# Delta-rule attention and a leaky-ReLU block on one Trainium2 core: corner blocks turned by VectorE transposes instead of DRAM bounces, inverses made for pairs of blocks, weights converted 768 columns at a time

## The chip, the cores and the metric

One core of one Trainium2 chip runs the whole program; the core has a matmul engine (PE, with its weight loads PEld), VectorE (DVE), ScalarE (ACT), GpSimd (POOL) and SyncE (SP), which issues most DMAs. The metric is the device time of one execution, in microseconds.

## The reference

```python
# q, k, v: (4, 8, 768, 48) float32; beta: (4, 8, 768); w_in (384, 2048), w_out (2048, 384) float64
k_n = k / (norm(k) + 1e-6)
for t in range(S):                        # S = 768 steps, state is 48 x 48 per sequence and head
    y[t]  = q[t] @ state
    v_old = k_n[t] @ state
    state = state + beta[t] * outer(k_n[t], v[t] - v_old)
x = y.transpose(0, 2, 1, 3).reshape(3072, 384)
h = x @ w_in
out = maximum(0.01 * h, h) @ w_out
```

## The kernel before, in words

The 768 steps are cut into 12 blocks of 64 steps, n = 0 to 11. In a block the recurrence over 64 steps is solved as a triangular system, so that all of it becomes matmuls; the 4 x 8 = 32 sequences and heads of a block are called lanes here. They are handled in two groups, g = 0 and 1. For each block there are these stages, each a Python generator, and `weave` writes their instructions in turns; a scheduler that plays the program against a timeline of its own then sets the final order on each engine.

- `gram(n)` (L175): loads keys and queries, transposed, into `kq` (two buffers, so g = 0 and g = 1 each have one), multiplies keys by keys and keys by queries on PE into `pg` (L201), copies the key products to `gs` on ACT (L205), and writes the masked query products to `rq` on DVE (L216). Each 64 x 64 product has two 32 x 32 diagonal corners and one corner below them. `gm` takes the lower corner (L220). The diagonal corners are written to DRAM (`gd`, 8 DMAs a block, L209) and read back into `L` (L224), which puts a lane and a half on each partition and the 32 x 32 corner along the free dimension.
- `inv(b)` (L272): inverts the corners on DVE. A memset clears `T` (L280), `norms` makes the key norms with a short Newton chain (L239 to L248) and scales `L` (L292), and `eliminate` (L253) goes through 31 columns, each with a multiply into `tmp` (L263) and a subtraction from `T` (L268), each in two parts. Blocks 0 and 1 are inverted together (64 + 64 partitions); from block 2 on each block alone uses the 128 partitions, with the columns split over two halves. The result goes back to the layout of the matmuls through DRAM: ACT makes a turned copy `Tt` (L299), DMAs write `td` and `tt` (L307, L308).
- `merge(n, g)` (L312): DMAs read `td` into `rt` and `tt` into `gm` (L318, L320); then two rounds of 32 x 32 matmuls, `pz` (L334) and `pu` (L342), give the lower corner of the inverse.
- `solve(n)` (L354): loads `rk`, `rv`, `rq` (L366, L367), scales `rv` by the norms on DVE (L388), and runs `pk` (L383), `pw` (L396), the state update `pc` (L404) and the output `py` (L414), each followed by copies on ACT. `columns(n)` (L435) turns the output into `px` (L443) and splits it into a high and a low part, `xh` on ACT and `xl` on DVE (L116).
- `ffn(n)` (L448): for each of 16 slices f of the 2048 columns 9 matmuls into `ph` (L468), leaky ReLU on ACT twice (`gh` L472, in place L473), the low part `gl` on DVE (L475), and 6 matmuls into `po` (L458), which run two slices behind. At the end `ob` is copied (L487) and stored (L490).
- `weights()` (L127): the weights come as float64. Each of 32 pieces of 384 columns (16 slices, two matrices) is turned into a high and a low part with two operations on ACT (L146, L160) and seven on DVE: four TENSOR_SCALARs (L148, L154, L156, L158) and three SCALAR_TENSOR_TENSORs (L155, L157, L161). Six pieces are written into the program ahead of the first inverse (KA = 6), the others behind it, and the last of them run beside the first block's `ffn`.

Every engine runs its instructions in the order given; DVE holds the inverse, the weights, `gl`, `rq` and more in one queue, and PE holds all matmuls in one queue. `weave` puts `solve(n+1)`, `inv(n+2)` and `gram(n+3)` beside `ffn(n)`.

Of the kernel before, what the change touches and what calls it, by code (L numbers as in the profile page):

```python
# [47 lines left out]
def delta_moe_kernel(ctx: ExitStack, tc, kqT, kv, qT, beta, cst, w_all, out, nblk):  # L48
# [65 lines left out]
    def split(src, hi, lo):  # L114
        nc.scalar.copy(hi, src)
        nc.vector.tensor_tensor(lo, src, hi.bitcast(F32), ALU.subtract)  # L116

    def load_w(k, gate=None):
        if k < 2 * NFC:
            raws[k] = raw = sb.tile([P, DO], U64, tag=f"w{k}", name=f"wr{k}", bufs=1)  # L120
            if gate:
                with behind(gate):
                    nc.vector.memset(raw[:, 0:1].bitcast(F32), 0.0)
            with behind("L"):
                nc.sync.dma_start(raw, w_all[:, k // 2, k % 2])

    def weights():  # L127
# [3 lines left out]
        for k in range(2 * NFC):  # L131
            f, x = k // 2, k % 2
            words = raws.pop(k).bitcast(F32).rearrange("p (n two) -> p two n", two=2)
            lo, hi = words[:, 0], words[:, 1]
            loi, hii = lo.bitcast(U32), hi.bitcast(U32)
            g = sb.tile([P, DO], F32, tag="cg", name=f"cg{k}", bufs=CB)
            r = sb.tile([P, DO], F32, tag="cr", name=f"cr{k}", bufs=1)
            gi, ri = g.bitcast(U32), r.bitcast(U32)

            def final():  # L140
                t = sb.tile([P, 2 * DO], F32R, tag=f"w{k}", name=f"w{k}", bufs=1)
                for e in range(2):
# [455 lines left out]
```

## Time and profile before

| What | Value |
|---|---|
| Runs of the kernel | 725.08, 725.47, 725.88 us; median 725.47 |
| Span of the profiled execution, first to last instruction | 722.7 us; the runs' median is 2.8 us above it |
| PE / DVE / ACT / POOL busy | 625.2 / 499.3 / 323.5 / 7.3 us |
| First matmul of `pz`, of `ph` | 77.37 us, 95.83 us |
| First copy of `ob` (end of block 0), of block 1 | 172.46 us, 212.73 us |
| Last copy of `ob` | 717.11 us |

Rows of a timeline give the start, the duration, the engine, the line, the operation, its tile and shape and how many were merged, and in brackets how long the engine had stood idle before and whom it waited for. Rows of a table by stage give the busy time of PE, PEld, DVE, ACT and POOL with the number of instructions, then the granted clock of the matmul engine, the DMA share and GB/s. Rows of the groups give line, engine, operation, tiles, shape and count, then busy time, the mean of one in ns, and the idle time before them.

### The profile page before, as it was taken

What the parts mean: (1) busy time and instruction counts of PE and PEld (TensorE: products, weight loads), DVE (VectorE), ACT (ScalarE), POOL (GpSimd) and SP (SyncE); (2) the same over time, 40 slices, a digit from 0 to 9 for tenths busy, and PEclk for the clock granted to TensorE, in tenths of its full rate; (3) what the DMA queues carried; (4) which work ended last, traced back from release to release, by engine and by line L of the source; (5) the groups of instructions that cost most, each with busy time, mean ns of one, the idle gap of its engine ahead of it and who ended that gap; (6) DMA issues with size and microseconds to landing.
All of it is one profiled execution on the core that took longest, in us unless ns stands there. A gap on an engine that the chain in (4) does not pass through costs nothing.

```text
span 722.7 us, 20972 instructions
## 1 busy us (share of the span) xinstructions
PE 625.2 (87%) x8296; PEld 580.9 (80%) x8296; DVE 499.3 (69%) x2222; ACT 323.5 (45%) x830; POOL 7.3 (1%) x12
## 2 busy tenths in 40 slices
PE   4200689978996999999999999999999999999996
PEld 4200569967995998988989999989989989999996
DVE  7988998999594856956955947847758559531211
ACT  3211554733453453554454544534634635544332
POOL 4000000000000000000000000000000000000000
PEclk9999978988997999999999999999999999999999
...
GB/s 239 102 271 107 177 206 131 59 115 23 46 14 128 85 57 164 4 68 154 3 98 124 3 128 95 15 136 73 32 142 49 50 129 2 68 24 2 3 20 23
DMA packets 130786, 60.91 MB, mean 84 GB/s; under 512 B 115392, under 2 KB 118592, under 8 KB 130688
## 3 DMA queue, kind: packets, MB, share of 16 engines
...
q8 instruction: 65, 1.06, 0.6%
...
## 4 chain that ended last, share of the span: by engine, by line
PE 65%; DVE 18%; DMA 7%; ACT 4%; SPq 3%; issue 3%; ACTq 0%; DVEq 0%
PE ph L468 26%; PE po L458 23%; PE pw L396 3%; PE pk L383 3%; DVE rq L216 3%; DMA tt<-T 3%; DVE rv L388 2%; DVE T L268 2%; PE pu L342 2%; DVE tmp L263 2%; DMA wr<-in_w_all 2%; PE py L414 2%; PE pz L334 2%; PE px L443 1%; SPq L307 1%
## 5 line engine op out<-in xcount | busy, mean ns | idle before, releaser
L468 PE MATMUL ph<-xh,w 128*128 128x256 f32 x1152 | 255.6, 295 | 11.4 <-DVE gl L475 8.2
L468 PEld LDWEIGHTS ph<-xh,w 128*128 128x128 f32 x1152 | 195.1, 192 | 22.5 <-DVE gl L475 11.4
L458 PE MATMUL po<-w,gh 128*128 128x384 f32 x768 | 188.0, 342 | 2.4 <-ACT gh L472 2.4
L475 DVE TENSOR_TENSOR gl<-ph,gh 128x256 fp32r<-128x256 f32 x192 | 80.4, 422 | 132.4 <-ACT ph L473 123.4
L468 PE MATMUL ph<-xl,w 128*128 128x256 f32 x576 | 165.9, 289 | 1.6 <-DVE xl L116 0.9
L472 ACT ACTIVATE gh<-ph 128x256 fp32r<-128x256 f32 x192 | 73.5, 383 | 171.2 <-PE ph L468 170.1
L458 PEld LDWEIGHTS po<-w,gh 128*128 128x128 f32 x768 | 132.3, 190 | 4.3 <-ACT gh L472 4.0
L458 PE MATMUL po<-w,gl 128*128 128x384 f32 x384 | 118.8, 343 | 1.5 <-DVE gl L475 1.4
L468 PEld LDWEIGHTS ph<-xl,w 128*128 128x128 f32 x576 | 110.7, 192 | 4.4 <-DVE xl L116 3.5
L268 DVE TENSOR_TENSOR T<-T,tmp 128x60 f32<-128x60 f32 (+35 forms) x661 | 112.0, 206 | 1.3
L263 DVE TENSOR_TENSOR tmp<-T,L 128x60 f32<-128x60 f32 (+35 forms) x661 | 111.9, 206 | 0.7
L473 ACT ACTIVATE ph<-ph 128x256 f32<-128x256 f32 x192 | 73.1, 380 | 0.0
L458 PEld LDWEIGHTS po<-w,gl 128*128 128x128 f32 x384 | 68.0, 191 | 2.4 <-DVE gl L475 1.9
L334 PE MATMUL pz<-rt,gm 32*32 32x32 f32 x768 | 19.7, 196 | 39.8 <-DMA rt<-td 39.7
L201 PE MATMUL pg<-kq 48*64 48x128 f32 x768 | 39.8, 313 | 13.2 <-DMA kq<-in_kqT 10.0
L334 PEld LDWEIGHTS pz<-rt,gm 32*32 32x32 f32 x768 | 15.9, 111 | 42.7 <-DMA rt<-td 39.9
L201 PEld LDWEIGHTS pg<-kq 48*64 48x64 f32 x768 | 32.0, 154 | 19.8 <-DMA kq<-in_kqT 10.8
L216 DVE TENSOR_TENSOR rq<-pg,csb 64x256 f32<-64x256 f32 x96 | 40.6, 423 | 2.2 <-ACT gs L205 0.5
L443 PE MATMUL px<-csb,ys 128*128 128x128 f32 x144 | 25.9, 299 | 8.1 <-DVE rq L216 5.1
L160 ACT CAST w<-cg 128x384 fp32r<-128x384 f32 x32 | 16.3, 511 | 36.8 <-DVE cr L157 26.5
L385 ACT ACTIVATE rt<-pk 48x512 f32<-48x512 f32 x44 | 26.1, 593 | 14.2 <-PE pk L383 13.4
L280 DVE MEMSET T<- 128x512 f32 (+1 forms) x11 | 5.8, 524 | 38.1 <-DMA tt<-T 37.9
...
## 6 DMA issues: line engine op xcount, KB each, us to landing
wr<-in_w_all SPq DMA_DIRECT2D x32, 384.0 KB, 4.9
kq<-in_kqT SPq DMA_DIRECT2D x44, 192.0 KB, 3.6
...
rk<-in_kv SPq DMA_DIRECT2D x24, 192.0 KB, 3.3
rv<-in_kv SPq DMA_DIRECT2D x24, 192.0 KB, 4.2
rq<-in_qT SPq DMA_DIRECT2D x24, 192.0 KB, 3.8
...
```

The source lines that it names most:

```text
L201: nc.tensor.matmul(ps[b][c * 64:(c + 1) * 64, p * 128:(p + 1) * 128], kq[r, c ^ b, p, 0], kq[r, c ^ b, p].rearrange("p x t -> p (x t)"), s ...
L216: nc.vector.tensor_tensor(qa[DN, c, b * NPAIR:(b + 1) * NPAIR], pv[b][r, 1], tri[r].rearrange("p (o t) -> p o t", o=1).broadcast_to([C, NP ...
L263: nc.vector.tensor_tensor(tv, t[:, :, j:j + 1].broadcast_to([P, k, w]), L[:, j, j + 1:].rearrange("p (o w) -> p o w", o=1).broadcast_to([P ...
L268: i = nc.vector.tensor_tensor(t, t, tv, ALU.subtract)
L334: nc.tensor.matmul(zv[h * 64:h * 64 + HC, u], gt[lo, l], t[lo, h, u, HC:], start=True, stop=True)
L385: nc.scalar.mul(t[UP, c], pv[c * 64:c * 64 + D], -1.0)
L443: nc.tensor.matmul(x[:, g * P:(g + 1) * P], ys[n, g][:, cc * P:(cc + 1) * P], eye, start=True, stop=True)
L458: i = nc.tensor.matmul(po[t][:, :DO], a[:, ts_], w[f], start=(f == 0 and k == 0), stop=(f == NFC - 1 and k == 2))
L468: nc.tensor.matmul(ph, a[f][:, cc * P:(cc + 1) * P], x[cc][e], start=(k == 0), stop=(k == 3 * NCC - 1))
L472: nc.scalar.activation(gh, ph, AF.Prelu, alpha=0.01)
L473: i = nc.scalar.activation(ph, ph, AF.Prelu, alpha=0.01)
L475: i = nc.vector.tensor_tensor(gl, ph, gh.bitcast(F32), ALU.subtract)
```

## The change

Blocks are now taken in pairs, b = 0 to 5, and what went through DRAM is turned on DVE.

- `gram(b)` handles two blocks, 64 partitions for each. ACT copies the key products of both to `S`; four VectorE transposes (`turn`, 32 partitions x 1024 elements each) bring the diagonal corners from `S` to `L`, and two copies of 32 x 1024 put the lower corners into `gm`, on DVE from the second pair on and on ACT for the first. For the first pair the key products of both groups come first, from separate `kq` tiles that lie in the space of weights not yet loaded, and the query products after them. For later pairs `kq` has one buffer of twice the size.
- `inv(b)` inverts the corners of both blocks at once, as blocks 0 and 1 were before, so there are 6 inverses of 31 columns in place of 11. `T` shares the buffer of `S`. 31 of its 33 steps are written beside an even block (from slot 5), the last two in slot 0 of the odd block.
- `merge(n)` takes three or four transposes of 32 x 1024 per block, two from `T` to `rt` and one to `gm`; the copies into `Tt` and the DMAs through `td` and `tt` are gone, as is the second copy of `gm` (L328). `rt` is one buffer for all blocks where there were two per block.
- The memsets of `rt` and `T` (the first one) and the identities in `rk` move from DVE to GpSimd.
- `weights()` takes 16 pieces of 768 columns. The middle bits are put together by 16-bit operations in place of the raw words (a copy, on ACT for 9 slices and on DVE for 7, and one TENSOR_SCALAR). On DVE stay four TENSOR_SCALARs and two SCALAR_TENSOR_TENSORs per slice. All pieces stand behind the first inverse. Each raw piece lies in the space of the next slice's result.

```diff
     def weights():
-        for k in range(2 * NFC):
...
-            nc.vector.tensor_scalar(gi, gi, 3, 0x3FFFF000, ALU.logical_shift_left, ALU.bitwise_and)
-            nc.vector.scalar_tensor_tensor(gi, hii, 0xC0000000, gi, ALU.bitwise_and, ALU.bitwise_or)
-            nc.vector.tensor_scalar(ri, hii, 0x1FF, 14, ALU.bitwise_and, ALU.logical_shift_left)
-            nc.vector.scalar_tensor_tensor(ri, loi, 18, ri, ALU.logical_shift_right, ALU.bitwise_or)
-            nc.vector.tensor_scalar(e.bitcast(U32), gi, 0xFF800000, None, ALU.bitwise_and)
+        for f in range(NFC):
...
+            if f < WU:
+                with behind("S"):
+                    nc.scalar.copy(part[:, 0], part[:, 1])
+            else:
+                with behind("x" if f >= WA else "inverse"):
+                    nc.vector.tensor_copy(part[:, 0], part[:, 1])
+            with behind("x" if f >= WA else "inverse"):
+                nc.vector.tensor_scalar(part[:, 1], part[:, 2], 0x1FF, None, ALU.bitwise_and)
+            with behind("x" if f >= WA else "inverse"):
+                nc.vector.tensor_scalar(g, g, HI_MIN, HI_MAX, ALU.max, ALU.min)
             nc.vector.tensor_scalar(gi, gi, 3, 0x3FFFF000, ALU.logical_shift_left, ALU.bitwise_and)
...
+            nc.vector.scalar_tensor_tensor(gi, hi, 0xC0000000, gi, ALU.bitwise_and, ALU.bitwise_or)
+            nc.scalar.copy(t[:, 0:2 * DO], g)
             nc.vector.tensor_scalar(e.bitcast(U32), gi, 0xFF800000, None, ALU.bitwise_and)
+            nc.vector.scalar_tensor_tensor(t[:, 2 * DO:], lo, 2.0 ** -36, e, ALU.mult, ALU.mult)
...
+        def kq(g):
+            t = sb.tile([P, 2, 2, GS, NPAIR, C], F32, tag="kq", name=f"kq{b}_{g}", bufs=1)
...
+        def turn():
+            for i, n in enumerate(ns):
+                for e in range(2):
+                    h = slice(e * HC, (e + 1) * HC)
+                    nc.vector.transpose(L[i * 64 + e * HC:i * 64 + (e + 1) * HC],
+                                            S[i * 64 + e * HC:i * 64 + (e + 1) * HC, :, h].rearrange("p l t -> p t l"))
+
+        def corners():
+            for i, n in enumerate(ns):
+                (nc.vector.tensor_copy if b else nc.scalar.copy)(gm[n][R0 + HC:P], S[i * 64 + HC:(i + 1) * 64, :, 0:HC])
...
     def inv(b):
...
-            eliminate(b, L, j, T, j + 1 if two else j // 2 + 1)
+            eliminate(b, L, j, T, j + 1)
             if j == HC - 2:
-                Tt = sb.tile([P, HC * HC], F32, tag="L", name=f"Tt{b}", bufs=2) if two else X[:, M * HC:]
-                Tt = Tt.rearrange("p (i m) -> p i m", m=M)
-                nc.scalar.copy(Tt.rearrange("p i m -> p m i"), T)
...
-    def merge(n, g, t):
...
+    def merge(n):
+
+        T, gt, a = Ts[n // 2], gm[n], n % 2 * 64
         for e in (1, 0):
-            dq(n).dma_start(t[R0 + e * HC:R0 + (e + 1) * HC].rearrange("p h u i -> p (h u) i")[:, :, e * HC:(e + 1) * HC],
-                            T[e, :, gl])
-        dq(n).dma_start(gt[0:HC], Tt[gl].rearrange("l i m -> i l m"))
+            nc.vector.transpose(rt[R0 + e * HC:R0 + (e + 1) * HC, :, e * HC:(e + 1) * HC].rearrange("p l i -> p i l"),
+                                T[a + e * HC:a + (e + 1) * HC].rearrange("p m i -> p i m"))
+        d = nc.vector.transpose(gt[0:HC].rearrange("p l m -> p m l"), T[a:a + HC])
...
-        weave(NF, (ff, NF, 0, NF), (wg, 2 * NFC * (n == 0), 0, 12), (sv, NS * (n + 1 < nblk), 2, 11),
-              (iv, NI * (n + 2 < nblk), 2, NF), (gg, NGR * (n + 3 < nblk), 11, 13))
+        a, z = n % 2 == 0 and n + 2 < nblk, n % 2 == 1 and n + 1 < nblk
+        weave(NF, (wg, NFC * (n == 0), 0, WB), (ff, NF, 0, NF), (sv, NS * (n + 1 < nblk), *SV[n % 2]),
+              (gg, NG * a, *GG), (iv, NA * a or (NI - NA) * z, *IV[n % 2]))
```

**The order on DVE at the end of the first inverse.** Before, conversion steps of the weights (`cg`, `cr`, `ce`, `w`) stand around the last subtraction into `T`:

```order
L148 TENSOR_SCALAR cg_864<-cg_864 128x384 [waits Activation_49]
L268 TENSOR_TENSOR T_335<-T_335,tmp_30_0_536 128x16 [waits DVE_49]
L154 TENSOR_SCALAR cg_818<-cg_818 128x384 [waits DVE_49]
L155 SCALAR_TENSOR_TENSOR cg_818<-wr_786,cg_818 128x384 [waits DVE_49]
L158 TENSOR_SCALAR ce_825<-cg_818 128x384 [waits DVE_49]
L161 SCALAR_TENSOR_TENSOR w_831<-cr_819,ce_825 128x384 [waits DVE_49]
```

Now the transposes into `rt` and `gm` and the scaling of `rv` by the norms `nt` follow it on the same engine, and the first conversion steps of the weights (`wr` is the raw piece, worked on in place) come behind those:

```order
L316 TENSOR_TENSOR T_292<-T_292,tmp_30_0_491 128x16 [waits DVE_49]
L348 STREAM_TRANSPOSE rt<-T_292 32x32x32 [waits DVE_49]
L350 STREAM_TRANSPOSE gm_88<-T_292 32x32x32
L426 TENSOR_TENSOR rv_83<-rv_83,nt_510 64x2x192 [waits DMAHW5_49,Activation_49]
L426 TENSOR_TENSOR rv_84<-rv_84,nt_510 64x2x192 [waits DMAHW0_49]
L147 TENSOR_SCALAR wr_264<-wr_264 128x768
L149 TENSOR_SCALAR cg_736<-cg_736 128x768
L150 TENSOR_SCALAR cg_736<-cg_736 128x768 [waits DVE_49]
```

The way out of the inverse has moved from DMA queues onto DVE, and all weight conversion stands behind it.

**The order on DVE where a new inverse is prepared.** Before, behind block 3's inverse, the memset of the next `T` stands in DVE's queue with waits for DMA queues (DMAHW), and the masked products `rq` behind it:

```order
L268 TENSOR_TENSOR T_2206<-T_2206,tmp_30_0_3031 128x8 [waits DVE_49]
L280 MEMSET T_3096 128x512 [waits DMAHW5_49,DMAHW4_49,DMAHW6_49,DMAHW1_49,DMAHW7_49,DMAHW0_49,Activation_49]
L216 TENSOR_TENSOR rq_77<-pg_0_0_2787,csb 64x256 [waits Activation_49]
L220 COPY gm_0_2786<-gs_0_2785 32x256 x2
L216 TENSOR_TENSOR rq_78<-pg_1_0_2851,csb 64x256 [waits Activation_49]
```

Now, in block 2, the last `rq` products of the pair, the four transposes and the two copies stand between two low parts `gl` of the feed-forward:

```order
L515 TENSOR_TENSOR gl_6_2790<-ph_72,gh_6_2789 128x256 [waits DVE_49,PE_49,Activation_49]
L377 TENSOR_SCALAR rt<-pu_1_2664 32x8x32 [waits Activation_49]
L265 TENSOR_TENSOR rq_80<-pg_1_1_0_2686,csb 64x256 [waits Activation_49]
L265 TENSOR_TENSOR rq_82<-pg_1_1_1_2687,csb 64x256
L205 STREAM_TRANSPOSE L_2462<-S_2461 32x1024 x4
L210 COPY gm_2459<-S_2461 32x1024
L210 COPY gm_2460<-S_2461 32x1024
L515 TENSOR_TENSOR gl_7_2825<-ph_73,gh_7_2824 128x256 [waits DVE_49,Activation_49]
```

The wait for DMA queues is gone from this place, and a run of DVE instructions without a `gl` has come.

**The order on SP where keys and queries are loaded.** Before, both tiles `kq_0` and `kq_1` of a block are asked for together, each in two DMAs of 48 x 1024, since each group has a buffer of its own:

```order
L184 DMA kq_0_3667<-in_kqT 48x1024 [waits DMAHW2_49,PE_49]
L224 DMA L_2783<-gd_2784 64x1024 [waits DMAHW5_49,DMAHW6_49,DMAHW4_49,DMAHW7_49,DMAHW3_49,DMAHW0_49]
L184 DMA kq_0_3667<-in_kqT 48x1024
L184 DMA kq_1_3670<-in_kqT 48x1024 [waits PE_49]
L366 DMA rv_83<-in_kv 64x768
```

Now (pair b = 3, made beside block 4) the second tile waits for PE, which has to be done with the first:

```order
L530 DMA out<-ob_1_3952 64x384 [waits DMAHW0_49,Activation_49]
L181 DMA kq_1_4061<-in_kqT 48x2048 [waits DMAHW2_49,PE_49]
L181 DMA kq_1_4061<-in_kqT 48x2048 [waits DMAHW3_49]
L181 DMA kq_0_5489<-in_kqT 48x2048 [waits DMAHW3_49,DMAHW4_49,DMAHW2_49,PE_49]
L283 DMA cb_7300<-in_beta 128x32 [waits DMAHW6_49,DVE_49]
```

The loads of 48 x 2048 carry the keys and queries of two blocks. On PE two slices of `ph` (18 matmuls) and 16 matmuls of `po` stand between the last reader of `kq_0_3976`, the first tile of this pair, and the first reader of `kq_1_4061`; beside block 2, for the pair b = 2, there are 12 matmuls of `ph` and 4 of `po`.

More of the change, by code (lines that the diff above doesn't have):

```diff
@@ L115, in split @@
         nc.scalar.copy(hi, src)
[L116 to L125, printed above, removed]
-    def weights():
-        for k in range(2 * NFC):
[L132 to L142, printed above, removed]
-                    (wi, wo)[x][e][f] = t[:, e * DO:(e + 1) * DO]
-                return (w[f] for w in (wi, wo)[x])
-            nc.scalar.activation(g, hi, AF.Abs)
-            with behind("inverse" if k >= KA else None):
-                i = nc.vector.tensor_scalar(g, g, HI_MIN, HI_MAX, ALU.max, ALU.min)
-            mark["work"] = i.ins
-            if k + WAHEAD >= WEARLY:
-                load_w(k + WAHEAD, "work")
-            e = sb.tile([P, DO], F32, tag="ce", name=f"ce{k}", bufs=1)
@@ L222, in gram @@
-            if g == NGR - 1:
-                for r in (i,) if len(NB[b0]) > 1 else (0, 1):
-                    d = nc.sync.dma_start(Lh[b0][r * 64:(r + 1) * 64].rearrange("l j i -> l (j i)"), gd.rearrange("l j i -> l (j i)"))
-                if n == 1:
-                    mark["L"] = d.ins
-                done.add((gram, n))
+            if (g, c) == steps[-1]:
+                turn()
+                corners()
+                done.add((gram, b))
             yield
@@ L268, in eliminate @@
             i = nc.vector.tensor_tensor(t, t, tv, ALU.subtract)
-        if b == 0:
-            mark["inverse"] = i.ins
     def inv(b):
-        for n in NB[b]:
-            need(gg, gram, n)
-        two = len(NB[b]) > 1
-        M = HC if two else HC // 2
-        X = sb.tile([P, HC * HC], F32, tag="T", name=f"T{b}", bufs=1)
-        T = X[:, 0:M * HC].rearrange("p (m i) -> p m i", m=M)
-        nc.vector.memset(T, 0.0)
+        if b:
+            need(gg, gram, b)
+        X = sb.tile([P, HC * HC], F32, tag="S", name=f"T{b}", bufs=1)
+        T = X.rearrange("p (m i) -> p m i", m=HC)
+        if b:
+            with behind("gl"):
+                nc.vector.memset(T, 0.0)
+        else:
+            nc.gpsimd.memset(T, 0.0)
         yield
@@ L324, in merge @@
         lo, r1 = slice(R0 + HC, P), slice(0, HC)
-        if len(NB[where[n][0]]) == 1:
-            r1 = slice(HC, 2 * HC)
-            with behind("h"):
-                nc.scalar.copy(gt[r1].rearrange("p l (m e) -> p l e m", e=2),
-                               gt[0:HC].rearrange("p l (e m) -> p l e m", e=2))
         with behind("po"):
@@ L352, in delta_moe_kernel, with fetch @@
     NSLOT = LD + 3
+    def fetch(n, g):
+        with behind("kq"):
+            for i, x in enumerate("kv"):
+                nc.sync.dma_start(of(x, n, g)[DN].rearrange("p h u t -> p (h u t)"), kv[n, g, i])
+            nc.sync.dma_start(of("q", n, g)[UP].rearrange("p h u t -> p (h u t)"), qT[n, g])
     def solve(n):
-        b, i = where[n]
+        b, i = n // 2, n % 2
         need(iv, inv, b)
@@ L387, in kt @@
                 us = slice(s * NPAIR, (s + 1) * NPAIR)
-                nc.vector.tensor_tensor(
+                with behind("inverse" if not n else None):
+                  nc.vector.tensor_tensor(
                     v[DN, :, us], v[DN, :, us],
```

263 lines of the change are left out of this document (159 added, 104 removed).

## The prediction

> **What bounds the kernel now.** I read the page's shares in 40 slices first, then the table by stage, then the timeline at the seams between stages.
>
> ```profile
> PE   4200689978996999999999999999999999999996
> ...
> DVE  7988998999594856956955947847758559531211
> ```
>
> PE is nearly idle in slices 2 to 4, not full in the next ten, and full from slice 14 on. DVE is the other way round.
>
> ```profile
> 43.40:64.60 21.20, 0.00 (x0) 0.00 (x0) 21.20 (x131) 0.00 (x0) 0.00 (x0) 1.00 0.49 112
> 64.60:77.40 12.80, 0.03 (x2) 0.03 (x3) 9.71 (x30) 5.53 (x9) 0.00 (x0) 1.00 1.05 220
> 77.40:95.80 18.40, 16.05 (x328) 14.66 (x328) 18.24 (x58) 11.42 (x24) 0.00 (x0) 1.00 0.72 194
> 95.80:172.50 76.70, 66.25 (x782) 59.38 (x783) 71.38 (x242) 39.94 (x103) 0.00 (x0) 0.84 0.43 104
> ...
> 212.70:233.50 20.80, 14.60 (x258) 12.90 (x256) 11.02 (x44) 7.92 (x20) 0.00 (x0) 0.75 0.56 106
> 233.50:640.60 407.10, 398.33 (x5556) 370.28 (x5555) 282.45 (x1396) 197.34 (x519) 0.00 (x0) 1.00 0.37 75
> ```
>
> The stages are the first inverse (21.2 us, DVE alone), the DRAM bounce after it (12.8 us, PE busy 0.03), the chain from `pz` to `ph`, block 0's feed-forward, and, after block 1's, a gap of 20.8 us; from 233.5 PE is busy 398 of 407 us. In block 0's feed-forward DVE is busy 71.4 of 76.7 us: it converts the weights there. The seams:
>
> ```profile
> 77.37 1.06 PE L334 MATMUL pz<-rt,gm 32*32 32x32 f32 x32 [39.74 <-DMA rt<-td]
> ...
> 172.46 0.86 ACT L487 COPY ob<-po 128x384 f32<-128x384 f32 x2
> ...
> 223.57 0.48 DVE L280 MEMSET T<- 128x512 f32 x1 [7.92 <-DMA tt<-T]
> 225.07 1.19 PE L443 MATMUL px<-csb,ys 128*128 128x128 f32 x4 [5.08 <-DVE rq L216]
> ...
> 233.52 0.38 ACT L472 ACTIVATE gh<-ph 128x256 fp32r<-128x256 f32 x1 [2.30 <-PE ph L468]
> 234.11 0.38 ACT L472 ACTIVATE gh<-ph 128x256 fp32r<-128x256 f32 x1
> ```
>
> At 77.37 PE waits for `td` to come back from DRAM. At 223.57 DVE's memset of `T` has stood 7.92 us behind the DMA that reads the old `T`; `rq` stands behind the memset, and PE waits for `rq`. So the change aims at places that set the end: the bounce, the weights, this memset.
>
> **Prices.** The rows nearest to the new operations:
>
> ```profile
> L475 DVE TENSOR_TENSOR gl<-ph,gh 128x256 fp32r<-128x256 f32 x192 | 80.4, 422 | 132.4 <-ACT ph L473 123.4 <-PE po L458 6.0
> L292 DVE TENSOR_TENSOR L<-L,cb 128x512 f32<-128x512 f32 x22 | 14.2, 687 | 0.1
> L155 DVE SCALAR_TENSOR_TENSOR cg<-wr,cg 128x384 uint32<-128x384 uint32 x32 | 17.4, 548 | 0.1
> L148 DVE TENSOR_SCALAR cg<-cg 128x384 f32<-128x384 f32 x32 | 11.2, 352 | 3.7 <-ACT cg L146 3.6
> L220 DVE COPY gm<-gs 32x256 f32<-32x256 f32 x48 | 13.8, 288 | 0.7
> L246 DVE RECIPROCAL rc<-sr 128x32 f32<-128x32 f32 x11 | 3.9, 351 | 0.3
> ```
>
> ```profile
> 33.00 0.36 DVE L156 TENSOR_SCALAR cr<-wr 128x384 uint32<-128x384 uint32 x1
> 33.27 0.35 DVE L158 TENSOR_SCALAR ce<-cg 128x384 uint32<-128x384 uint32 x1
> 33.54 0.18 DVE L239 TENSOR_SCALAR sr<-L 128x32 uint32<-128x32 uint32 x1
> ```
>
> From 32 to 384 columns a TENSOR_SCALAR grows from 0.18 to 0.35 us, so 768 cost about 0.54; I take 0.55. Two-operand operations grow by 0.265 per 256 columns (422 to 687 ns), so a SCALAR_TENSOR_TENSOR of 768 costs 0.548 + 0.398, say 0.95. A copy of 32 x 1024 lies between: from the 0.288 of 256 columns, at a TENSOR_SCALAR's slope, 0.67; I take 0.69. The 16-bit operations are not in the trace; 0.55 is taken, between 0.35 (a 384-column one) and 0.95 (two-operand rate), since they are copies and TENSOR_SCALARs. Each instruction here starts some 0.08 us before the former ends (33.00 + 0.36 against 33.27), so a sum of durations overstates by 0.08 for each.
>
> The transposes are not in the trace either. At the two-operand slope, one of 32 x 1024 costs 0.687 + 2 x 0.265 = 1.22. The low end is a copy's 0.69. The high end is 2.45: on 128 x 32 a RECIPROCAL takes 0.351 where a TENSOR_SCALAR takes 0.18, so an operation can cost twice its neighbour. I take 1.22: both sides' elements go through at the commonest rate of the rows, and the doubled rows are of one special operation. [...]
>
> **From the start to `pz`.** Keys land as before. The key products of the first pair are 128 matmul records of half the width:
>
> ```profile
> 4.02 1.97 PE L201 MATMUL pg<-kq 48*64 48x128 f32 x16 [4.02 <-DMA kq<-in_kqT]
> ...
> 16.14 2.89 PE L201 MATMUL pg<-kq 48*64 48x128 f32 x32 [5.05 <-DMA kq<-in_kqT]
> ...
> 424.12 1.10 PE L201 MATMUL pg<-kq 48*64 48x128 f32 x32
> ```
>
> Here 90 ns each cold and 34 warm; I take 50 for the half width, 6.4 us, which ends at 10.4 (range 9 to 16, since all could cost 90). The last copy to `S` adds 0.7, four transposes 4.9 (16.0), the eight masked products, 64 x 512 in size, 8 x 0.61 = 4.9, the norms some 3 (about a dozen operations on 128 x 32 at 0.18 to 0.35) and the scaling 1.5: 25.4. The inverse has the form of the first one, 21.2: 46.6. Three transposes, 3.7: `pz` at about 50.5, where it was 77.37. Weights that stood ahead of the first inverse (KA = 6) have left this stretch.
>
> **Block 0.** On DVE now stand, from the end of those transposes to the last `gl` of block 0: weights 16 x (4 x 0.55 + 2 x 0.95) = 65.6; seven copies 3.85; 12 operations on `rv`, 16 `rq`, 16 `gl` and 6 `xl`, with these rows:
>
> ```profile
> L388 DVE TENSOR_TENSOR rv<-rv,nt 64x384 f32<-64x384 f32 x48 | 23.8, 555 | 7.9 <-ACT nt L360 7.7
> L216 DVE TENSOR_TENSOR rq<-pg,csb 64x256 f32<-64x256 f32 x96 | 40.6, 423 | 2.2 <-ACT gs L205 0.5
> 43.45 0.28 DVE L263 TENSOR_TENSOR tmp<-T,L 128x31 f32<-128x31 f32 x2
> 78.00:170.00 92.00, 79.57 (x1083) 71.58 (x1078) 86.52 (x283) 49.44 (x121) 0.00 (x0) 0.87 0.50 125
> ```
>
> That is 6.7 + 6.8 + 6.8 + 2.5; further the second pair's four transposes 4.9, two corner copies 1.4, `T` memset 0.9 (the 128 x 512 one took 0.48), norms and scaling 4.5, block 1's three transposes 3.7, small copies 1.7, and 26 operations of the next elimination at some 0.2 us, 5.6. Sum 115; less 0.08 x 190 instructions, 99.8. DVE won't be full: in the last row above 5.5 of 92 us are idle, so I add 6. Block 0's last `gl` comes at 50.5 + 99.8 + 6 = 156.5, some 13.5 us before the like point of before (172.46, the copy behind it, less 2.4). The gain of 27 at `pz` is thus halved, since DVE's queue, not the chain, ends block 0: weights that had been converted ahead of `pz` now come after it. PE is covered by this and can lose there without price. If the 16-bit operations took 0.95, their 23 would add 9 us here; at 0.35 they take 4.6 off.
>
> **Block 1.** The elimination is interleaved with f0 to f10. A slice at PE's own rate:
>
> ```profile
> 712.74 0.38 ACT L472 ACTIVATE gh<-ph 128x256 fp32r<-128x256 f32 x1 [1.45 <-PE ph L468]
> ...
> 714.85 0.38 ACT L472 ACTIVATE gh<-ph 128x256 fp32r<-128x256 f32 x1 [1.45 <-PE ph L468]
> ```
>
> 11 x 2.11 = 23.2 leads to 179.7; block 2's first four transposes stand ahead of a `gl` on DVE, 4.9: 184.6. Then `pz`, `pu` and the last slices, about 8 (three slices 6.3 and copies), and of the 18.4 us chain the 13 behind `pu`, and 2.5 of waits at the rate of 6 in 92: first `gh` of block 2 at 208 to 209, I take 208.5, against 233.52. The memset's wait of 7.92 has no successor, for no DMA reads `T`. Gain so far 25.0.
>
> **Blocks 2 to 9.** The same mark in later blocks:
>
> ```profile
> 593.54 0.38 ACT L472 ACTIVATE gh<-ph 128x256 fp32r<-128x256 f32 x1
> ...
> 640.55 0.38 ACT L472 ACTIVATE gh<-ph 128x256 fp32r<-128x256 f32 x1
> ...
> 685.55 0.38 ACT L472 ACTIVATE gh<-ph 128x256 fp32r<-128x256 f32 x1
> ```
>
> Seven blocks from 234.11 to 593.54: 51.35 each, with a gram beside them; 47.0 for block 9 without one; 45.0 for block 10. In all 406.4 for blocks 2 to 9. Now an even block carries two grams: 47.0, and 128 products at 34 ns, 4.4. Two costs come on top. First, the second `kq` tile waits for PE to be done with the first:
>
> ```profile
> kq<-in_kqT SPq DMA_DIRECT2D x44, 192.0 KB, 3.6
> ...
> wr<-in_w_all SPq DMA_DIRECT2D x32, 384.0 KB, 4.9
> ```
>
> Two loads of 384 KB take between 3.6 and 9.8 (2 x 4.9, one behind the other); I take 6, near the like-sized row. PE has 34 matmuls between, 34/15 of a slice, 4.8: wait 1.2. Beside block 2 it has 16, 2.25: wait 3.75. Behind these DMAs on SP only loads stand that are wanted later. Second, a run of DVE instructions without `gl`: four `rq`, four transposes, two copies, 7.95 less 0.8; `po` runs two slices (4.2) behind, so PE may lack 3 us less what `pk` and `pw` fill: 1.4. An even block is 54.0, block 2 2.5 more. An odd block is 47.0 with 0.5 for its transposes on DVE, which has time. Sum 4 x 54.0 + 2.5 + 4 x 47.5 = 408.5, that is 2.1 more than before. Half the eliminations bring nothing here: DVE was idle 125 of 407 us already. The end, blocks 10 and 11, is unchanged.
>
> [...]
>
> ```profile
> 158.00:162.00 4.00, 3.32 (x13) 3.06 (x13) 3.84 (x14) 0.66 (x2) 0.00 (x0) 0.50 0.09 27
> 162.00:166.00 4.00, 1.40 (x6) 1.30 (x6) 3.97 (x13) 0.51 (x1) 0.00 (x0) 0.50 0.00 0
> ```
>
> Where PE had little to do, its granted clock was 0.50. [...]
>
> **Sum.** 722.7 - 25.0 + 2.1 = 699.8 of span; the runs' median lies 2.8 above the span: **702.5 us**.
>
> **Rivals.** (1) Transposes twice as dear, 2.45 each. 18 of them stand on DVE's way to block 2 (four, three, four, three, four): 18 x 1.23 = 22. In the steady state a pair's `turn` and merges lengthen runs without `gl` by about 4.9 for each pair with a gram, 20 in all. That is 744, slower than before. It decides from where the gain of 23 is used up: 34 transposes (18 and 4 x 4) cost it at 0.68 more each, 1.9 us. For it: nothing in the trace transposes. Against: no row of 64 columns or more runs that slowly for each element. Chance 0.06. [...] (2) The reload and the run without `gl` cost PE 3 to 5 us in each of the four even blocks, above what I have: 12 to 20 more, 715 to 722, I take 717. For it: loads of `kq` beside others may be near 9.8. Against: the mean of 3.6 for the half size. Chance 0.13. (3) The transposes run at a copy's rate: 18 x 0.53 = 9.5 off, and the even blocks have neither wait, 4 x 1 off: 689. Chance 0.12. (4) DVE's sum in block 0 does not set its end and the bounce's 27 us all come through: that needs conversion to be cheaper than any row; it is within (3).
>
> **How the numbers follow.** The forecast, 692 to 712, takes in the key products (up to 6), the 16-bit operations (9 more, 5 less) and the loads, with chance 0.69. The range 688 to 719 adds (3) and most of (2). A measurement of this kernel can tell about 0.2%, 1.5 us, from no change. Faster: the forecast, (2) and (3), 0.94, of which 0.01 goes to "same" for several costs at their high ends together: 0.93; slower 0.06 from (1); same 0.01.
>
> **What would show it.** Right: `pz` near 50, the last `gl` of block 0 near 157, the first `gh` of block 2 near 208, STREAM_TRANSPOSE of 32 x 1024 near 1.2 us, TENSOR_SCALARs of 768 near 0.55, pairs of blocks near 101.5 us apart, and a PE wait for `kq` of 1 to 4 us per pair. Wrong: transposes above 1.9 us, or pairs above 105, or a first `gh` of block 2 after 220; and below 100 per pair the waits I charge are hidden.

## The result and the profile after

The changed kernel takes 782.94 us (median of 4 runs, 781.9 to 784.52), the kernel before 725.67 beside it: ratio 1.079, 95% interval 1.077 to 1.081. It is slower by 57 us; the forecast was 702.5 us, faster by 23, with 688 to 719 as the range. The profiled execution has a span of 782.0 us.

The shares in 40 slices, of the kernel after:

```profile
PE   4026887889899898999898999798999898999997
...
DVE  5999999999653899335998324898325898332121
...
PEclk9998567979998899899999998998999898999999
```

PE is no longer full from slice 14 on: in every six slices, the length of a pair of blocks, a 7 or 8 stands twice, and the granted clock dips as well. The table by stage says how much. Its stages are the first merge, the chain to the first `gh`, block 0, block 1, blocks 2 to 9, and block 10:

```profile
49.05:54.80 5.75, 1.07 (x32) 0.96 (x32) 5.69 (x3) 0.73 (x2) 0.00 (x0) 1.00 1.01 297
54.80:86.06 31.26, 23.13 (x331) 20.53 (x333) 29.89 (x40) 14.95 (x28) 0.00 (x0) 0.77 0.28 87
86.06:175.20 89.14, 75.72 (x752) 65.67 (x753) 87.85 (x176) 42.20 (x88) 0.00 (x0) 0.75 0.16 39
175.20:232.84 57.64, 54.05 (x707) 50.82 (x705) 40.70 (x127) 22.80 (x60) 0.00 (x0) 0.97 0.18 42
232.84:698.94 466.10, 432.80 (x5556) 403.33 (x5554) 301.36 (x876) 180.67 (x485) 0.00 (x0) 0.93 0.16 37
698.94:743.27 44.33, 44.09 (x565) 41.98 (x564) 9.69 (x23) 18.26 (x49) 0.00 (x0) 1.00 0.04 10
```

The first 233 us take as long as before (232.84 against 233.52 at the first `gh` of block 2), though `pz` comes 26 us earlier. In the kernel before, the first `gh` of block 10 is this row:

```profile
639.13 0.38 ACT L472 ACTIVATE gh<-ph 128x256 fp32r<-128x256 f32 x1 [1.41 <-PE ph L468]
```

Between these two marks blocks 2 to 9 took 405.6 us before (the prediction's row to 640.60 ends at the second `gh` of block 10) and take 466.1 now: the whole loss is there. PE stands idle for 33.3 of the 466.1 us (8.8 before), 24.5 us more, and is busy for 36.0 us longer with the same matmuls, at a granted clock of 0.93 where it was 1.00. The last blocks are unchanged. PE's waits in this stretch (total, times, longest):

```profile
PE ph L508 <- DVE gl L515: 19.8, 8, 4.4
PE pu L373 <- DVE gm L350: 8.1, 4, 2.2
PE pg L257 <- DMA kq<-in_kqT: 5.0, 4, 2.0
```

So 27.9 of the 33.3 us are waits for VectorE and 5.0 waits for `kq`.

The groups of VectorE instructions that the forecast priced:

```profile
L348 DVE STREAM_TRANSPOSE rt<-T 32x1024 f32<-32x1024 f32 x24 | 51.6, 2148 | 16.8 <-PE pw L434 16.3
L205 DVE STREAM_TRANSPOSE L<-S 32x1024 f32<-32x1024 f32 x24 | 46.9, 1956 | 0.5
L350 DVE STREAM_TRANSPOSE gm<-T 32x1024 f32<-32x1024 f32 x12 | 22.7, 1890 | 0.3
L147 DVE TENSOR_SCALAR wr<-wr 128x768 uint16<-128x768 uint16 x16 | 15.4, 1041 | 0.1
L155 DVE SCALAR_TENSOR_TENSOR w<-wr,ce 128x768 fp32r<-128x768 uint32 x16 | 15.2, 951 | 0.1
L149 DVE TENSOR_SCALAR cg<-cg 128x768 f32<-128x768 f32 x16 | 8.9, 559 | 0.1
L145 DVE COPY wr<-wr 128x768 uint16<-128x768 uint16 x7 | 6.4, 1073 | 0.0
```

The 768-column operations cost what was forecast (0.559 and 0.951). The transposes cost 1.89 to 2.15 us, not 1.22, and the 16-bit operations 1.04 and 1.07, not 0.55.

What a pair of blocks loses is seen on a timeline of blocks 6 and 7. First VectorE and PE around the four transposes of the next pair:

```profile
489.79 1.75 DVE L265 TENSOR_TENSOR rq<-pg,csb 64x256 f32<-64x256 f32 x4 [0.63 <-ACT S L261]
491.55 7.80 DVE L205 STREAM_TRANSPOSE L<-S 32x1024 f32<-32x1024 f32 x4
499.38 1.39 DVE L210 COPY gm<-S 32x1024 f32<-32x1024 f32 x2
500.80 0.76 DVE L515 TENSOR_TENSOR gl<-ph,gh 128x256 fp32r<-128x256 f32 x2
```

```profile
501.28 0.39 PE L508 MATMUL ph<-xh,w 128*128 128x256 f32 x1 [4.44 <-DVE gl L515]
...
544.90 0.58 PE L508 MATMUL ph<-xh,w 128*128 128x256 f32 x1 [1.29 <-DVE gl L515]
```

For 11 us VectorE makes no `gl` (489.79 to 500.80); PE uses up its two slices of lookahead and then waits 4.44 us. At the end of the inverse four transposes (536.45 to 544.4) do the same again. One further place of the pair waits for `kq`, 1.21 us up to 477.15. The granted clock (the third number from the end of a row) after this wait and after the transposes:

```profile
476.00:479.00 3.00, 1.85 (x38) 1.82 (x40) 0.20 (x1) 0.60 (x2) 0.00 (x0) 0.82 0.02 5
479.00:482.00 3.00, 3.00 (x33) 2.94 (x29) 2.94 (x8) 0.77 (x4) 0.00 (x0) 0.50 0.00 0
...
497.00:500.00 3.00, 0.00 (x0) 0.00 (x0) 2.96 (x3) 0.00 (x0) 0.00 (x0) 1.00 0.00 0
500.00:503.00 3.00, 1.72 (x10) 1.72 (x11) 2.76 (x8) 0.00 (x0) 0.00 (x0) 0.80 0.00 0
503.00:506.00 3.00, 3.00 (x16) 3.00 (x16) 2.04 (x9) 1.07 (x4) 0.00 (x0) 0.63 0.00 0
```

PE is busy again, but the granted clock is 0.50 from 479 to 482 and 0.63 from 503 to 506: slow stretches follow these waits. The trace's clock record has eleven such stretches at 0.50 in blocks 2 to 9, 65 us in all: three begin at a wait for `kq`, four at the transposes into `L`, four at the end of an inverse.

### The profile page after: what moved, and what is told of

Its sections match the earlier page's. It is cut to its first block, busy times and chain, and to the rows that moved or that the text cites. A ratio compares the mean times of both kernels' runs of the same rounds, so it can differ in the third digit from the quotient of the medians.

```text
span 782.0 us, 19886 instructions
## 1 busy us (share of the span) xinstructions
PE 673.5 (86%) x8424; PEld 624.9 (80%) x8424; DVE 521.0 (67%) x1410; ACT 315.4 (40%) x766; POOL 12.5 (2%) x18
## 4 chain that ended last, share of the span: by engine, by line
PE 62%; DVE 27%; issue 5%; DMA 4%; ACT 1%; SPq 0%; ACTq 0%; DVEq 0%
PE ph L508 24%; PE po L498 21%; DVE L L205 4%; DMA kq<-in_kqT 4%; PE pg L257 3%; DVE gm L350 3%; PE py L452 2%; DVE rt L348 2%; DVE T L316 2%; PE pw L434 2%; PE pc L442 2%; DVE tmp L311 2%; PE px L481 2%; DVE cg L152 2%; PE pk L420 2%
## 5 line engine op out<-in xcount | busy, mean ns | idle before, releaser
L508 PE MATMUL ph<-xh,w 128*128 128x256 f32 x1152 | 270.2, 308 | 28.9 <-DVE gl L515 23.6
L508 PEld LDWEIGHTS ph<-xh,w 128*128 128x128 f32 x1152 | 209.0, 206 | 38.9 <-DVE gl L515 25.2
L508 PE MATMUL ph<-xl,w 128*128 128x256 f32 x576 | 173.8, 302 | 0.1
L508 PEld LDWEIGHTS ph<-xl,w 128*128 128x128 f32 x576 | 119.4, 207 | 1.7 <-issue 0.8
L316 DVE TENSOR_TENSOR T<-T,tmp 128x110 f32<-128x110 f32 (+35 forms) x366 | 76.6, 246 | 0.3
L311 DVE TENSOR_TENSOR tmp<-T,L 128x110 f32<-128x110 f32 (+35 forms) x366 | 76.4, 246 | 0.1
L348 DVE STREAM_TRANSPOSE rt<-T 32x1024 f32<-32x1024 f32 x24 | 51.6, 2148 | 16.8 <-PE pw L434 16.3
L265 DVE TENSOR_TENSOR rq<-pg,csb 64x256 f32<-64x256 f32 x80 | 33.8, 422 | 28.9 <-ACT S L261 27.5
L205 DVE STREAM_TRANSPOSE L<-S 32x1024 f32<-32x1024 f32 x24 | 46.9, 1956 | 0.5
L257 PEld LDWEIGHTS pg<-kq 48*64 48x64 f32 x640 | 30.7, 148 | 11.7 <-issue 9.1
L452 PE MATMUL py<-rv,rq 128*64 128x48 f32 x768 | 31.3, 230 | 4.3 <-issue 4.2
L373 PEld LDWEIGHTS pu<-zs,gm 32*32 32x32 f32 x768 | 17.3, 114 | 19.9 <-issue 16.1
```

The lines of the kernel that those rows point to most:

```text
L205: nc.vector.transpose(L[i * 64 + e * HC:i * 64 + (e + 1) * HC], S[i * 64 + e * HC:i * 64 + (e + 1) * HC, :, h].rearrange("p l t -> p t l"))
L257: nc.tensor.matmul(bank[y][i * 64:(i + 1) * 64, p * 128:(p + 1) * 128], t[r, 0, i, c ^ y, p], t[r, :, i, c ^ y, p], start=True, stop=True)
L265: nc.vector.tensor_tensor(of("q", n, g)[DN, c, y * NPAIR:(y + 1) * NPAIR], view[y][r, 1], tri[r].rearrange("p (o t) -> p o t", o=1).broadc ...
L311: nc.vector.tensor_tensor(tv, t[:, :, j:j + 1].broadcast_to([P, k, w]), L[:, j, j + 1:].rearrange("p (o w) -> p o w", o=1).broadcast_to([P ...
L316: i = nc.vector.tensor_tensor(t, t, tv, ALU.subtract)
L348: nc.vector.transpose(rt[R0 + e * HC:R0 + (e + 1) * HC, :, e * HC:(e + 1) * HC].rearrange("p l i -> p i l"), T[a + e * HC:a + (e + 1) * HC ...
```

## The experiments

Theory A: runs on VectorE that hold transposes starve PE, and the clock drops after each. Theory B: the second `kq` tile, which waits for PE, is the main loss. Theory C: the inverse of a pair, packed into one block, delays `gl`. For block 0 the question was whether the 16-bit work sets its end. Results of all runs, with the stretch of blocks 2 to 9 from the first `gh` of block 2 to that of block 10 (us; clock is the granted clock in that stretch). The diffs below are excerpts; `...` stands for the other lines.

| Run | Time | first `gh` of block 2 | blocks 2 to 9 | PE idle there | clock |
|---|---|---|---|---|---|
| before | 723 to 726 | 233.5 | 405.6 | 8.8 | 1.00 |
| after | 782.9 | 232.8 | 466.1 | 33.3 | 0.93 |
| no_reload | 768.5 | 237.7 | 446.7 | 26.6 | 0.96 |
| bounce | 752.8 | 225.3 | 441.9 | 22.3 | 0.97 |
| spread | 758.1 | 237.3 | 435.8 | 21.4 | 0.98 |
| warm | 807.7 | 234.1 | 484.2 | 27.5 | 0.93 |
| no_u16 | 765.6 | 217.3 | 466.7 | 31.1 | 0.93 |
| kqhalf | 767.3 | 235.2 | 448.4 | 26.3 | 0.95 |
| bounce_kq | 735.4 | 229.7 | 423.7 | 12.6 | 0.99 |
| spread_kq | 740.3 | 233.3 | 423.1 | 16.6 | 1.00 |
| best | 737.4 | 228.1 | 421.2 | 11.9 | 0.99 |
| best_clamp | 739.1 | 229.8 | 422.7 | 14.3 | 0.99 |
| probes | 783.9 | 234.8 | 464.3 | 35.5 | 0.94 |
| double | 795.7 | 241.8 | 470.0 | 36.1 | 0.94 |
| plain | 765.3 | 225.5 | 450.5 | 11.7 | 0.95 |
| plain3_spread_kq | 737.4 | 228.2 | 421.0 | 5.7 | 1.00 |
| turn3_spread_kq | 726.3 | 234.1 | 409.3 | 5.8 | 1.00 |
| turn3_wu12 | 729.3 | 236.1 | 412.4 | 6.1 | 0.99 |
| turn3_no_u16 | 703.7 | 208.4 | 409.6 | 6.0 | 1.00 |

**no_reload**, the second load left out:

```diff
-            if not c:
+            if not c and not g:
                 t = kq(g)
```

> Leaves out the load of the second key-query tile of every pair from b = 1 on (both groups use the first tile, so the products of group 1 are of the wrong data); nothing else changes. Theory A (runs of transposes on VectorE starve the matmul engine, and its clock is halved after each such gap): only the four waits for kq go, 5.0 us in the trace, and some 2 us of slow clock behind each: 768 to 774 us. Theory B (the single kq buffer is the main loss of the steady state): 745 us or less.

768.5 us: theory A's number, and B falls as the main cause. But blocks 2 to 9 gain 19.4 us, more than the 5 us of waits: PE's idle time falls by 6.7 us and its busy time by 12.6, as the clock rises from 0.93 to 0.96. The first two blocks lose 5 us in exchange, which was not looked into.

**bounce**, most transposes of later pairs back to DRAM:

```diff
-                turn()
+                nc.sync.dma_start(L..., gd...)      # after 8 writes of S to gd
...
-            nc.vector.transpose(rt[...], T[...])
+                nc.sync.dma_start(rt[...], Td[n // 2][...].rearrange("l m i -> m l i"))
```

> From the second pair on, the four transposes into L and the two into rt go back to DRAM bounces; the two into gm stay on VectorE, so 8 of 10 transposes per pair leave it; the inverses by pairs, the single kq buffer and the weights stay as changed. Theory A: idle time and slow clock between 232.8 and 698.9 us go down by two thirds or more, 730 to 750 us, granted clock of that stretch above 0.97. Theory B (kq) and theory C (the inverse of a pair packed into one block delays the low parts gl): 772 us or more, since neither is touched.

752.8 us, 24 us less in blocks 2 to 9, less than expected. The reason stands in VectorE's rows of this run:

```profile
481.13 0.91 DVE L335 MEMSET T<- 128x1024 f32 x1 [5.76 <-DMA gd<-S]
481.96 0.36 DVE L535 TENSOR_TENSOR gl<-ph,gh 128x256 fp32r<-128x256 f32 x1
482.38 0.39 PE L528 MATMUL ph<-xh,w 128*128 128x256 f32 x1 [3.08 <-DVE gl L535]
```

`T` shares the buffer of `S`, as in the changed kernel; now that DMAs read `S`, the memset waits for them, and `gl` stands behind it. It is the stall of the kernel before, back in another place.

**spread**, transposes of later pairs two by two:

```diff
-                turn()
                 corners()
+                for x in range(5):
+                    yield
+                    if x > 2:
+                        with behind("gl"):
+                            turn((2 * x - 6, 2 * x - 5))
```

(the merges likewise; solve and inverse in later slots). In this run block 1's transposes also overwrite `rt` before block 0 has used it, mended in spread_kq.

> Every transpose stays on VectorE; from the second pair on they are issued two at a time, each two behind a low part gl of a later slice, and the merge, solve and inverse streams are moved by some slots to make room. Theory A: runs on VectorE without a gl are halved to some 4 us, which the two slices of lookahead cover: 740 to 760 us. If the amount of VectorE work counts and not its order, or theory B or C holds: 775 to 790 us.

758.1 us. VectorE does as much work as after in blocks 2 to 9 (301.6 against 301.4 us), yet they take 30 us less: the order of the work counts, not its amount.

**warm**, useless matmuls ahead of the gaps (one of three places):

```diff
+            if n > 2 and n % 2 and not g:
+                for _ in range(10):
+                    nc.tensor.matmul(p[:, GU * D:512], eye, csb[:, 0:P], start=True, stop=True)
```

> Adds 24 useless matmuls of 128 x 128 x 128 (about 0.3 us each, 7 us a pair, 30 us in all) on the matmul engine just ahead of the places where it idles in each pair: 10 ahead of pw of the odd block, 8 ahead of pz of the even one, 6 ahead of the products of the second kq tile. Theory A with the clock as its larger half: the added work fills gaps, the clock stays near 1.0 and the time falls, 755 to 772 us. If gaps cost only their own length: 780 to 786 us. If there are no gaps that the work can fill: 800 us or more.

807.7 us, the number given for no gaps that the work can fill. The gaps behind the transposes into `L` became shorter (2.07 for 4.44 us), but 18 us were added in blocks 2 to 9 and the clock stayed at 0.93: behind a gap of 2.07 us, up to 511.76, two `ph` matmuls still took 0.63 us (from 512.58) where two took 0.40 later (from 516.98). A likely reason, not shown, is that work ahead of a gap delays the very products that VectorE turns next. So this run does not part the clock's share from the idle share.

**no_u16**, the 16-bit work of VectorE left out:

```diff
-                    nc.vector.tensor_copy(part[:, 0], part[:, 1])
...
-                nc.vector.tensor_scalar(part[:, 1], part[:, 2], 0x1FF, None, ALU.bitwise_and)
```

> Leaves out the 16-bit work on VectorE in the weight conversion (16 TENSOR_SCALARs and 7 copies, 1.04 and 1.07 us each in the trace, 24 us in all), so the low parts of the weights are wrong. If VectorE's queue sets the end of block 0 (theory A and the forecast's step), the first gh of block 1 comes 20 to 24 us earlier and the total falls to 758 to 764 us. If the chain through the matmul engine sets it, less than 8 us: above 774.

Block 1 starts 16.5 us earlier (158.11 against 174.62), and 17 us come off in all: between the two numbers, nearer to VectorE's queue as the bound.

**kqhalf**, loads of half a tile in turn in the same space:

```diff
-            t = sb.tile([P, 2, 2, GS, NPAIR, C], F32, tag="kq", ..., bufs=1)
+            t = kqb[:, v]...      # v = 0, 1: half of the heads
```

> The kq space of one tile is cut in two halves that are loaded in turn (each with the keys and queries of half the heads of both blocks), so that a load runs while the products of the other half are made; nothing is left out and the transposes stay. If the load behind the matmul engine is worth what the kernel without the second load showed: 764 to 772 us. If the slow clock there comes from the many small products and not from the wait: 778 to 783 us.

767.3 us, as no_reload, and with nothing left out. The waits for `kq` cost some 18 us in blocks 2 to 9, the slow clock behind them included.

**bounce_kq**, bounce and kqhalf together, and `T` cleared by GpSimd:

```diff
-                nc.vector.memset(T, 0.0)
+        nc.gpsimd.memset(T, 0.0)
```

> Bounce and kqhalf together, and the memset of T moved to GpSimd, since in bounce it stood 5.8 us in VectorE's queue behind the DMAs that read S. Theory A (three places where the matmul engine starves in each pair: the runs of transposes, the kq load, and with the bounce the memset): 712 to 728 us, granted clock of blocks 2 to 9 at 0.99. If the packing of the inverse into one block costs as well (theory C): 732 us or more.

735.4 us, above theory A's range and in theory C's. **spread_kq**, spread and kqhalf together, with the order of the first pair mended:

> Spread and kqhalf together (all ten transposes of a pair on VectorE, two behind a gl; the order of the first pair mended). Theory A: 735 to 745 us, since spread alone still waited for kq and for two long runs of the inverse. If the two savings overlap: 750 us or more.

740.3 us, as expected. Both leave some 18 us in blocks 2 to 9.

**best** (all 16-bit copies on ScalarE) and **best_clamp** (a clamp on GpSimd), on top of bounce_kq:

> Bounce_kq with all 16 of the 16-bit copies of the weights on ScalarE (9 before), 7 x 1.07 = 7.5 us less on VectorE in block 0. If VectorE's queue sets the end of block 0: 726 to 731 us. If ScalarE, which then holds the copies ahead of the first gh, delays block 0 instead: 735 us or more.

> Best with the clamp of the weights' exponents (a TENSOR_SCALAR of 768, 0.56 us on VectorE) on GpSimd for 12 of the 16 slices, 6.7 us less on VectorE. If GpSimd's work does not disturb VectorE: 4 to 7 us below best. If the two slow each other down, or the hop to GpSimd delays the chain of a slice: at best's time or above.

737.4 and 739.1 us: no gain. In best the first `gh` comes at 93.06 us (86.95 in bounce_kq) and block 1 starts at the same time, which fits the expectation that ScalarE's copies ahead of the first `gh` take back what VectorE saves. Why the clamp on GpSimd brings nothing was not looked into.

**probes**, extra VectorE instructions at the end of the kernel:

```diff
+    nc.vector.transpose(xb[q], xa[q])
+    nc.vector.transpose(xb[q], tu(xa[q]))     # tu: "p l t -> p t l"
...
```

> The changed kernel, with eleven extra VectorE instructions at its end whose results nobody uses: transposes of 32 x 1024 with plain views, with a turned view on the input, on the output and on both, of 32 x 512 and of 128 x 1024 with plain views, a turned copy, and 16-bit operations on plain and on strided data. If the turned view is what makes a transpose cost 1.9 us in place of the forecast's 1.22: the plain one takes 1.1 to 1.3. If the transpose itself is that slow: 1.8 to 2.0 plain too. If a transpose is paid by instruction and not by partitions, 128 x 1024 costs the same as 32 x 1024. The 16-bit ones: if the stride makes them slow, plain ones take 0.3 to 0.55 and strided ones 0.95 to 1.1.

The rows, in the order of the text above (L580 to L592, without the two 16-bit copies):

```profile
L580 DVE STREAM_TRANSPOSE xb<-xa 32x1024 f32<-32x1024 f32 x1 | 1.2, 1233 | 0.0
L581 DVE STREAM_TRANSPOSE xb<-xa 32x1024 f32<-32x1024 f32 x1 | 2.1, 2056 | 0.0
L582 DVE STREAM_TRANSPOSE xb<-xa 32x1024 f32<-32x1024 f32 x1 | 2.0, 2025 | 0.0
L583 DVE STREAM_TRANSPOSE xb<-xa 32x1024 f32<-32x1024 f32 x1 | 1.9, 1943 | 0.0
L584 DVE STREAM_TRANSPOSE xb<-xa 32x512 f32<-32x512 f32 x1 | 0.7, 689 | 0.0
L585 DVE STREAM_TRANSPOSE xb<-xa 128x1024 f32<-128x1024 f32 x1 | 1.2, 1214 | 0.0
L586 DVE COPY xb<-xa 32x1024 f32<-32x1024 f32 x1 | 1.1, 1065 | 0.0
L589 DVE TENSOR_SCALAR xb<-xa 128x768 uint16<-128x768 uint16 x1 | 0.4, 361 | 0.0
L590 DVE TENSOR_SCALAR xb<-xa 128x768 uint16<-128x768 uint16 x1 | 0.6, 609 | 0.0
```

A transpose with plain views takes 1.233 us, the forecast's price. A turned view on either side makes it 1.94 to 2.06. All 128 partitions cost what 32 do, 1.214 and 1.233 us. 16-bit work costs 0.361 plain, 0.609 with every second element, and 1.04 in the kernel, where every fourth is taken (L147 above).

**double**, the four transposes into `L` issued twice:

> The four transposes into L are issued twice in the five pairs from b = 1 on (the second set gives the same result; the scheduler puts one to four low parts between the two sets): 7.8 us more on VectorE in each pair, 39 in all. Theory A: the longer runs are paid by the matmul engine: 800 to 825 us. If VectorE's idle time in these blocks covers them: 783 to 792 us.

795.7 us, between the two. Blocks 2 to 9 lose 3.9 us for 30 us of VectorE work; low parts stand between the two sets, so it is another sign that order counts and not amount. The other 9 us are lost ahead of block 2.

**plain**, `S` and `gm` laid out so that six of ten transposes of a pair have plain views:

```diff
-        S = sb.tile([P, HS, C], F32, tag="S", ...)
+        S = sb.tile([P, C, HS], F32, tag="S", ...)
-            gm[n] = sb.tile([P, HS, HC], F32, tag="gm", ...)
+            gm[n] = sb.tile([P, HC, HS], F32, tag="gm", ...)
```

> The changed kernel with S kept as columns by lanes and gm as rows by lanes, so that the four transposes into L and the two into gm of a pair have plain views on both sides (the two into rt of each block keep turned views); ScalarE's copies into S now write turned. Theory A with the view as the cause of the price: these six take 1.2 to 1.25 us in place of 1.9 to 1.96, each pair has 4.2 us less on VectorE in its two longest runs, and the time falls by 16 to 26 us: 757 to 767. If ScalarE's turned copies delay the products instead: 775 us or more.

765.3 us, as expected; the rows L206 and L351 of this run show 1236 and 1232 ns. So the price of six of the ten transposes is back at the forecast's, and blocks 2 to 9 still take 450.5 us: the price alone is not the miss. PE is idle for 11.7 us only, yet the clock is 0.95. It falls also where the rows show PE busy throughout, without a gap; spread_kq, with gaps of 1.44 and 1.48 us in each pair, stays at 1.00 behind them. First two rows of plain, then two of spread_kq around such a gap:

```profile
469.75:473.16 3.41, 3.41 (x97) 2.96 (x96) 0.84 (x2) 0.81 (x3) 0.00 (x0) 1.00 0.00 0
473.16:476.57 3.41, 3.41 (x16) 3.41 (x17) 2.75 (x5) 1.67 (x4) 0.00 (x0) 0.50 0.80 159
```

```profile
497.00:500.00 3.00, 1.56 (x12) 1.24 (x11) 2.94 (x12) 0.55 (x2) 0.00 (x0) 1.00 0.54 124
500.00:503.00 3.00, 3.00 (x23) 3.00 (x22) 3.00 (x17) 1.14 (x4) 0.00 (x0) 1.00 0.03 7
```

The 97 matmuls are nearly all small ones (`pu` and `pg`); around the gap of spread_kq stand the large ones of the feed-forward.

**plain3_spread_kq**, the plain views with spread_kq's order and halves:

> Spread_kq with the plain views, and the four transposes into L made by three instructions (one over all 128 partitions, then the two corners that it gets wrong). Theory A: 712 to 728 us, since spread_kq (740 us) loses some 3 to 4 us in each of five pairs; below 723 us it would be faster than both kernels. If what is left in spread_kq is the packed inverse (theory C) and not the transposes: 735 us or more.

737.4 us, which spoke for theory C. But PE was busy 415 of the 421 us, so it did not wait for any inverse. Two of its groups in that stretch, first of this run, then of the kernel before:

```profile
L398 PE MATMUL pu<-zs,gm 32*32 32x32 f32 x512 | 20.3, 219 | 0.0
L390 PE MATMUL pz<-rt,gm 32*32 32x32 f32 x512 | 19.5, 219 | 0.0
```

```profile
L342 PE MATMUL pu<-zs,gm 32*32 32x32 f32 x512 | 13.0, 193 | 0.0
L334 PE MATMUL pz<-rt,gm 32*32 32x32 f32 x512 | 13.0, 193 | 0.0
```

The weights loaded from the turned `gm` cost PE 14 us more. **turn3_spread_kq** puts `gm` back (plain views for the transposes into `L` alone), **turn3_wu12** has three more copies on ScalarE:

> Plain3_spread_kq with gm back as lanes by rows, so that the matmul engine loads its weights for pz and pu without a stride; the two transposes into gm of a pair have a turned view again and the corner copies read S turned. If the strided weight loads are what was left there (pz and pu took 20 us each between 228 and 649 us, 13 before): 723 to 729 us, level with the kernel before. If the packed inverse is what is left (theory C): 735 us or more.

> Turn3_spread_kq with 12 of the 16-bit copies on ScalarE in place of 9, 3.2 us less on VectorE in block 0. If VectorE's queue still sets the end of block 0: 2 to 3 us below turn3_spread_kq. If ScalarE's earlier load delays the first gh by as much: no difference within 1.5 us.

726.3 us, as expected, ratio to the kernel before 1.0006 (0.998 to 1.0033); turn3_wu12 729.3, ratio 1.0046 (1.002 to 1.0071), neither of its two numbers and not looked into. Blocks 2 to 9 take 409.3 us with an inverse packed into one block as in the other versions: theory C is not needed.

**turn3_no_u16**, turn3_spread_kq with the edit of no_u16:

> Turn3_spread_kq without the 16-bit work on VectorE (so the low parts of the weights are wrong), to close the account of the forecast. Turn3_spread_kq has blocks 2 to 9 at 409 us, as forecast, and is late only up to block 2 (234 us against 208.5). If the 16-bit work at twice its forecast price is most of that: first gh of block 2 at 214 to 220, 708 to 713 us in all. If something else holds block 0: 720 us or more.

703.7 us, ratio 0.971 (0.968 to 0.974), better than expected. The first `gh` of block 2 of this run:

```profile
208.42 0.39 ACT L532 ACTIVATE gh<-ph 128x256 fp32r<-128x256 f32 x1 [0.56 <-PE ph L528]
```

The forecast was 208.5 there and 702.5 in all, but with 23 16-bit operations at 0.55 in it, 12.7 us, and this run has none: that the two numbers meet is luck. The three transposes behind the first inverse end at 56.25 here, where the forecast has 50.5, and from the last `gl` of block 0 (148.38) to this row it is 60.0 us, where the forecast has 52.0. No version that computes the whole result came below the kernel before.

## Why the prediction was wrong

- **What bounds the kernel before**: right. The end of block 0 is VectorE's, the steady blocks are PE's.
- **From the start to `pz`**: 50.5 forecast, 51.10 measured, right in sum but not in its parts, which is luck. The four transposes took 7.83 us for 4.9, and the inverse ended at 49.05 for 46.6; but `pz` needs only the first of the three transposes behind it and starts when that is done. The forecast counts block 0 from the end of all three, and that comes at 54.79, 4.3 us late:

```profile
52.90 1.89 DVE L350 STREAM_TRANSPOSE gm<-T 32x1024 f32<-32x1024 f32 x1
```

- **Block 0**: the terms "768 columns" were right to 0.01 us. The 16-bit term was mis-sized: 16 x 1.04 + 7 x 1.07 in place of 23 x 0.55, 11.5 us more, above even the range's 9. Seven transposes at 0.75 more are another 5. With the 4.3 us of above, and 3 less of idle time on VectorE than the 6 that the forecast added, the last `gl` of block 0 comes at 173.70 where the forecast had 156.5. no_u16 and turn3_no_u16 show the 16-bit part: with all 24.1 us of it left out, block 1 starts 16.5 and 25.2 us earlier.
- **Block 1**: from there to the first `gh` of block 2 it is 59.1 us, where the forecast has 52.0. PE alone is busy for 55.6 us of it and waits 3.6 us for VectorE, so the forecast's sum of slices and a chain had left out work of PE; which part is not shown.
- **The price of a transpose**: this is the step that failed first. The price of 1.22 was that of the operation with plain views, as probes shows; all transposes of the change have a view whose neighbouring elements lie 128 or 256 bytes apart. The trace of before had a row with such a view, and it was passed over: ScalarE's copy into `Tt`.

```profile
64.64 2.01 ACT L299 COPY Tt<-T 128x1024 f32<-128x1024 f32 x1 [22.78 <-DVE T L268]
```

  It took 2.01 us for 1024 elements, where a row of 128 x 256 on ScalarE (0.38) would suggest 1.5 at most. Nearest was not the engine or the operation, but the view. In probes the view alone took one fp32 transpose from 1.233 to 2.056 us. The 16-bit work, at 8 bytes from element to element, took 1.04 us in the kernel, and 0.361 with the plain views of probes. The runs show the price of these views; its cause is not shown.
- **Rival 1** had the direction and, at 1.9 us each, its own point of no gain. It would have given 725 there, and 730 at the measured mean of 2.02 us, not 783. What it lacked is the next point.
- **Blocks 2 to 9**: "an even block 54.0, an odd one 47.5" failed; they took some 60.6 and 55.9, 466.1 us for the forecast's 408.5. This is 58 of the 80 us by which the forecast missed. The forecast set each wait against the cover of two slices and charged what was left over. For `kq` that was 1.2 us a pair, 3.75 in the first; the four waits add up to 5.0 us, so this term was large enough. For the runs without a `gl` it was 1.4 us in an even block and 0.5 in an odd one; PE waits 7.0 us a pair for VectorE, since runs of 8 to 11 us without a `gl` came twice. For the clock the sum to 702.5 has no term; PE is busy for 9.0 us a pair longer than before, 36.0 us in all, which is more than the 24.5 us of added idle time. The clock accounts for most of it, by an estimate: the 65 us at 0.50 are worth up to 32 us. The clock of 0.50 followed the gap of 4.44 us, but also one of 1.21 us between small products (`pg`, `pn`, `pz`) and, in plain, 3.41 us without any gap, while 1.44 us between large products in spread_kq left it at 1.00; so the length of a gap alone does not tell when it comes. Small products around it fit better, and the runs do not settle it.
- With order, halves and plain views the same blocks take 409 us, next to the forecast's 408.5. So that time can be had, but it does not confirm the forecast's terms: 14.9 us of the 408.5 are waits, and this kernel has three repairs that the forecast did not ask for. What the idle time and the slow clock are worth alone stays open: warm did not part them, and they do not go together in every run (plain 11.7 us and 0.95, spread_kq 16.6 us and 1.00).
